# Four small changes at the start, middle and end of a fused attention and Fourier-mix kernel: row 0 loaded apart, batch 0 cast on two engines, batch 2 turned by DMA, the last tile stored 384 and 128 wide

## The chip, the cores and the metric

One core of one Trainium2 chip. The metric is the device time of one execution in microseconds (us). Before: 315.28 us median of 3 runs (315.26 to 315.30). The profile's span is about 1.8 us shorter than that time; times inside a profile count from the start of its span. All comparisons below use runs of the fast state (granted clock 0.99 to 1.00).

## The reference

```python
# x (8, 8, 512, 64) = batch, head, row, d; state (8, 8, 32, 64); w_ch1 (512, 2048); w_ch2 (2048, 512)
scores = x @ state^T / 8;  xread = softmax(scores) @ state        # 512 rows
scores2 = state @ x^T / 8; sread = softmax(scores2) @ x           # 32 rows
x = concat([xread, sread], rows) -> (8, 576, 512)                 # heads side by side
mixed = real(fft(fft(x, axis=1), axis=2))
u  = x + mixed
un = (u - mean(u)) / sqrt(var(u) + 1e-6)
out = u + relu(un @ w_ch1) @ w_ch2
# ... (cut: drawing of the inputs)
```

## The kernel before: what the change and the argument touch

The kernel writes one schedule for all engines by hand. A batch goes through these stages: load `x` and cast it to bfloat16 (`xin`), turn (transpose) it and the state (`xT`, `sT`), scores and exponentials, the reads (`XF`, `XR`, `XL`), the Fourier sums (`gp`, `yp`), `u` and its statistics, the turned `u` (`unT`), then the two matmul layers (`ph`, `po`), which are most of the time, and the store. Stages of the next batch are woven between the matmuls of the present one.

```python
    def load_x(b):                       # on SyncE's queue, two of batch 0's on ACT's
        ...
        for n, (ps, si, rows) in enumerate((
            (slice(0, 128), 2, xb[256:384]),
            (slice(0, 128), 0, xb[1:129]),
            (slice(0, 128), 1, xb[129:257]),
            (slice(0, 128), 3, xb[384:512]),
            (slice(0, 1), 2, xb[0:1]),           # overwrites partition 0 of the first load
        )): ...
    def cast_x(b):
        if b == 0:
            for si in (0, 1, 3, 2):
                nc.scalar.copy(t[:, si, 1:513], xs[:, si, :])
        else:
            nc.gpsimd.tensor_copy(t[:, :, 1:513], xs)
    # ... (cut)
    load_state(0, 1); load_x(0); load_state(1, 2); load_x(1)
    nc.sync.dma_start(out=s_dram[2:]..., in_=state[2:, :, ::-1, :]...)   # reversed state to HBM
    load_state(2, B, s_dram)                                            # SyncE waits for it here
    # ... (cut)
    x_by_dma, u_by_dma = 3, 2            # from which batch on x, and u, are turned by DMA
        def turn_x(g):
            if b >= x_by_dma:
                for si in ((0, 1), (3, 2))[g]:
                    nc.sync.dma_start_transpose(out=xT[:, :, 128 * si:128 * si + 128], in_=xin[:, si, 1:513])
                return
            ... # 8 transposes on TensorE, then
            (nc.vector.tensor_copy if b == 0 or g == 0 else nc.scalar.copy)(xT[:, 2 * g:2 * g + 2, :], ...)
        def turn_u(k, r):
            if b >= u_by_dma:
                nc.sync.dma_start_transpose(out=unT[:, :, col:col + 128], in_=ub[k, r])
                return
            ...
    # layer 2, the last tile of the last batch
                h = q // 2
                cols = slice(256 * h, 256 * h + 256)
                ... # 16 matmuls for each half, then DVE writes ot and SyncE stores it
    def warm(n):                         # idle matmuls: identity x identity into a tile nobody reads
        t = psF.tile([128, 512], F32, name="warm", tag="c")
        for i in range(n):
            nc.tensor.matmul(t[:, 0:128], lhsT=ident, rhs=ident, start=(i == 0), stop=(i == n - 1))
    # ... (cut) in the opening, while TensorE has nothing else to do:
    weave((warmed(s0[:1], 4) + warmed(s0[1:3], 2) + s0[3:], 0, 1), ...)
    weave((warmed(r0, 4), 0, 1), ..., ([lambda: warm(44)], 1, 1))
```

The softmax here doesn't subtract the row's maximum and nothing guards it: scores larger than these inputs give would overflow.

## Time and profile before

| | before |
|---|---|
| time | 315.28 us |
| span of the profile | 313.6 us |
| matmuls of TensorE, busy | 2320, 300.5 us (96%) |
| layer 1 of batch 0 starts | 28.65 us |
| first Fourier sum over d (yp) of batch 1 | 54.27 us |
| layer 1 of batch 2 starts | 91.85 us |
| start of the last 32 matmuls, end of the span | 306.51, 313.6 us |

Read it as a program that is bound by TensorE from about 42 us on, with a start of 42 us in which several engines hand work to each other, and an end of 3.5 us that no engine can overlap. The prediction shows the lines.

### The profile page before, as it was taken

What the parts mean: (1) busy time and instruction counts of PE and PEld (TensorE: products, weight loads), DVE (VectorE), ACT (ScalarE), POOL (GpSimd) and SP (SyncE); (2) the same over time, 40 slices, a digit from 0 to 9 for tenths busy, and PEclk for the clock granted to TensorE, in tenths of its full rate; (3) what the DMA queues carried; (4) which work ended last, traced back from release to release, by engine and by line L of the source; (5) the groups of instructions that cost most, each with busy time, mean ns of one, the idle gap of its engine ahead of it and who ended that gap; (6) DMA issues with size and microseconds to landing.
All of it is one profiled execution on the core that took longest, in us unless ns stands there. A gap on an engine that the chain in (4) does not pass through costs nothing.

```text
span 313.6 us, 5980 instructions
## 1 busy us (share of the span) xinstructions
PE 300.5 (96%) x2320; PEld 172.4 (55%) x2320; DVE 187.0 (60%) x445; ACT 138.5 (44%) x269; POOL 74.8 (24%) x170
## 2 busy tenths in 40 slices
PE   5878999999999999999999999999999999999995
PEld 5666997544544555456645554455445544555444
DVE  8796874968677593873817774686569563100012
ACT  6698765645543443243442444234533333333300
POOL 8658497320240040300600024002200131000000
PEclk9999999999999999999999999999999999999999
DMA  7997999466464925348434343631333034303155
GB/s 142 194 197 136 202 179 213 106 119 144 79 113 88 220 48 135 81 106 155 95 72 100 86 100 83 129 75 52 81 73 67 33 84 98 73 34 67 38 133 132
DMA packets 111532, 34.22 MB, mean 109 GB/s; under 512 B 102928, under 2 KB 107280, under 8 KB 111504
## 3 DMA queue, kind: packets, MB, share of 16 engines
q1 hardware_dynamic: 100784, 28.08, 43.1%
q0 software_dynamic: 4224, 4.19, 8.3%
q10 hardware_dynamic: 6496, 1.57, 2.4%
q8 instruction: 18, 0.29, 0.4%
q14 instruction: 10, 0.08, 0.1%
HBM read 22.43 MB, written 14.02 MB: 116 GB/s over the span
## 4 chain that ended last, share of the span: by engine, by line
PE 81%; DVE 12%; ACT 2%; DMA 2%; issue 1%; SPq 0%; DVEq 0%; ACTq 0%
PE po L762 32%; PE ph L696 29%; PE gp L576 3%; PE ph L706 3%; DMA xs<-in_x_dram 2%; DVE U L546 2%; DVE st L316 1%; PE yp L542 1%; PE po L754 1%; PE yp L541 1%; PE xfp L434 1%; PE xrp L434 1%; PE gp L580 1%; PE esp L409 1%; DVE XF L443 1%
## 5 line engine op out<-in xcount | busy, mean ns | idle before, releaser
L762 PE MATMUL po<-w,hT 128*128 128x512 bf16 x496 | 125.0, 379 | 0.0
L698 ACT ACTIVATE hT<-ph 128x512 bf16<-128x512 f32 x112 | 66.9, 597 | 123.7 <-PE ph L696 121.8
L696 PE MATMUL ph<-unT,w 128*128 128x512 bf16 x448 | 114.6, 379 | 0.4 <-DVE ot L727 0.3
L696 PEld LDWEIGHTS <-w 128*128 128x128 bf16 x576 | 51.1, 98 | 48.8 <-issue 1.3
L762 PEld LDWEIGHTS <-hT 128*128 128x128 bf16 x496 | 47.0, 98 | 44.3
L727 DVE SCALAR_TENSOR_TENSOR ot<-po,rstd,U 128x512 f32<-128x512 f32 (+1 forms) x33 | 24.2, 732 | 52.6 <-PE po L762 48.1
L586 POOL COPY GL<-G 128x128 bf16<-128x128 bf16 x8 | 2.4, 296 | 113.2 <-ACT G L584 113.2
L546 DVE TENSOR_TENSOR U<-yp,XR 128x512 f32<-128x512 f32 x16 | 10.9, 682 | 22.8 <-PE yp L542 22.8
L316 DVE BATCH_NORM_STATS2 st<-U 128x6 f32<-128x512 f32 x32 | 21.9, 683 | 0.1
L322 POOL TENSOR_TENSOR rstd<-mv,epst 128x1 f32<-128x1 f32 x34 | 7.1, 210 | 61.4 <-DVE mv L318 61.4
L323 POOL TENSOR_TENSOR rstd<-rstd,mhalf 128x1 f32<-128x1 f32 x34 | 20.9, 615 | 2.7
L584 ACT CAST G<-gp 128x288 bf16<-128x288 f32 x31 | 12.2, 397 | 12.0 <-PE gp L580 6.9
L706 PE MATMUL ph<-unT,w 128*128 128x128 bf16 x256 | 15.9, 219 | 0.7 <-ACT unT L620 0.7
L782 PE MATMUL warm<-ident 128*128 128x128 bf16 x152 | 12.8, 237 | 3.8 <-POOL ident masks.py:199 3.4
L706 PEld LDWEIGHTS <-w 128*128 128x128 bf16 x256 | 15.0, 98 | 0.9 <-issue 0.8
L782 PEld LDWEIGHTS <-ident 128*128 128x128 bf16 x152 | 11.1, 107 | 4.7 <-POOL ident masks.py:199 3.4
L576 PEld LDWEIGHTS <-XQ 128*128 128x128 bf16 x96 | 8.8, 98 | 8.8 <-DVE XQ L506 2.3
L136 POOL CAST xin<-xs 128x2048 bf16<-128x2048 f32 x7 | 13.2, 1891 | 0.3 <-issue 0.2
L610 DVE TENSOR_SCALAR ub<-U,mv 128x512 bf16<-128x512 f32 x24 | 12.3, 510 | 1.0 <-DVE mv L318 0.2
L434 PEld LDWEIGHTS <-ET 128*128 128x128 bf16 x80 | 7.0, 98 | 9.1 <-DVE XF L443 1.6
L443 DVE TENSOR_TENSOR XR<-xrp,rs 128x512 bf16<-128x512 f32 x16 | 11.1, 695 | 1.0 <-POOL XR L276 0.4
L708 ACT ACTIVATE hT<-ph 128x512 bf16<-128x512 f32 x16 | 9.3, 598 | 3.9 <-PE ph L706 3.9
(190 smaller groups left out, 356.5 us busy)
## 6 DMA issues: line engine op xcount, KB each, us to landing
xs<-in_x_dram SPq DMA_DIRECT2D x30, 256.0 KB, 5.3
w<-in_moe_w_ch_dram POOLq DMA_DIRECT2D x8, 512.0 KB, 11.6
out_dram<-ot SPq DMA_DIRECT2D x15, 256.0 KB, 3.6
r_dram<-ot SPq DMA_DIRECT2D x14, 256.0 KB, 2.2
out_dram<-r_dram SPq DMA_DIRECT2D x14, 256.0 KB, 3.7
xs<-in_x_dram ACTq DMA_DIRECT2D x2, 256.0 KB, 4.0
l_dram<-ot SPq DMA_DIRECT2D x2, 256.0 KB
r_dram<-ot ACTq DMA_DIRECT2D x2, 256.0 KB
```

The costliest lines, as they stand in the source:

```text
L316: nc.vector.bn_stats(st6, u)
L323: nc.gpsimd.tensor_tensor(rstd, rstd, mhalf, op=ALU.pow)
L434: nc.tensor.matmul(ph[:, 0:260], lhsT=ET[:, g, c0:c0 + 128], rhs=rhs, start=True, stop=True)
L443: nc.vector.tensor_tensor(ov, in0=p[ps, :, 0:256].rearrange("p g (h d) -> p g h d", d=D), in1=rs[ps].unsqueeze(3).to_broadcast([n, 2, 4, D ...
L546: nc.vector.tensor_add(u.rearrange("p (k r) -> p k r", r=2), p.rearrange("p (r k) -> p k r", r=2)[:, 0:u.shape[1] // 2, :], x.rearrange("p ...
L576: nc.tensor.matmul(p[:, 0:NM], lhsT=XQ[:, j, c, :], rhs=tab[c], start=(c == 0), stop=(c == 2 and j != 2))
L696: nc.tensor.matmul(ph[:, o:o + n], lhsT=w1[:, c, f * 128:(f + 1) * 128], rhs=un_of[key][:, c, :], start=(c == 0), stop=(c == DC - 1))
L698: nc.scalar.activation(hT[:, per * i:per * i + per, :].rearrange("p a b -> p (a b)"), ph, AF.Relu, scale=-1.0 if key in flipped else 1.0)
L706: nc.tensor.matmul(ph[:, o:o + 128], lhsT=w1[:, c, f * 128:(f + 1) * 128], rhs=un_of[key][:, c, 128 * r:128 * r + 128], start=(c == 0), st ...
L727: nc.vector.scalar_tensor_tensor(ot[:, cols], in0=po_of[i][:, 0:cols.stop - cols.start], scalar=rstd, in1=u[:, cols], op0=ALU.mult, op1=AL ...
L762: nc.tensor.matmul(po_of[i], lhsT=h_of[key][:, f, i * 128:(i + 1) * 128], rhs=w2[:, f, :], start=(f == 0), stop=(f == FC - 1))
L782: nc.tensor.matmul(t[:, 0:128], lhsT=ident, rhs=ident, start=(i == 0), stop=(i == n - 1))
```

## The change

Its intent: (1) row 0 of `x` need not wait for the landing of another load; (2) two engines cast batch 0; (3) TensorE, DVE and ACT are spared the turning of batch 2's `x` and state; (4) the last store, which nothing hides, is made smaller.

```diff
-            (slice(0, 128), 2, xb[256:384]),
+            (slice(32, 128), 2, xb[288:384]),
             ...
-            (slice(0, 1), 2, xb[0:1]),
+            (slice(2, 32), 2, xb[258:288]),
+            (slice(0, 2), 2, xb[0:258:257]),
@@
-            for si in (0, 1, 3, 2):
+            for si in (0, 1, 3):
                 nc.scalar.copy(t[:, si, 1:513], xs[:, si, :])
+            nc.gpsimd.tensor_copy(t[:, 2, 1:513], xs[:, 2, :])
@@
-    x_by_dma, u_by_dma = 3, 2
+    x_by_dma, u_by_dma = 2, 2
@@
-            (nc.vector.tensor_copy if b == 0 or g == 0 else nc.scalar.copy)(
+            (nc.vector.tensor_copy if g == (b == 0) else nc.scalar.copy)(
@@
-                h = q // 2
-                cols = slice(256 * h, 256 * h + 256)
+                cols = slice(0, 384) if q < 2 else slice(384, 512)
@@  (the width of the matmuls follows cols)
-    ... [last_sines, exp_again, last_loads, load_x3,
+    ... [last_sines, exp_again, last_loads, turned[2], load_x3,
-    ... (scores_next, 0.26, 0.9) ...
+    ... (scores_next, 0.4, 1) ...
```

More of the change, by code (lines that the diff above doesn't have):

```diff
@@ L753, in step @@
                 for f in range(8 * (q % 2), 8 * (q % 2) + 8):
-                    nc.tensor.matmul(po_of[i][:, 0:256], lhsT=h_of[key][:, f, i * 128:(i + 1) * 128], rhs=w2[:, f, cols],
+                    nc.tensor.matmul(po_of[i][:, 0:cols.stop - cols.start], lhsT=h_of[key][:, f, i * 128:(i + 1) * 128], rhs=w2[:, f, cols],
                                      start=(f == 0), stop=(f == FC - 1))
@@ L797 @@
     turns1, copies1, s1 = s1[0], s1[1:4], s1[4:]
-    for step in (warmed(t0[:2], 2) + [alternate, more_loads] + warmed(t0[2:4], 2) + [last_sines, exp_again, last_loads, load_x3,
+    for step in (warmed(t0[:2], 2) + [alternate, more_loads] + warmed(t0[2:4], 2) + [last_sines, exp_again, last_loads, turned[2], load_x3,
             t0[4], t0[8], W(6), turns1, t0[5], W(10), t0[7], copies1[0], copies1[1], t0[6], copies1[2],
@@ L804 @@
     weave((L[11:], 0, 0.25), (t1, 0.2, 1), ([M[i] for i in (0, 4, 1, 5, 2, 6, 3, 7, 8, 9)], 0.33, 0.99),
-          ([lambda: state_blocks(3, B, nc.gpsimd.tensor_copy)], 0.35, 0.35), (scores_next, 0.26, 0.9), ([lambda: load_x(4)], 0.6, 0.6))
+          ([lambda: state_blocks(3, B, nc.gpsimd.tensor_copy)], 0.35, 0.35), (scores_next, 0.4, 1), ([lambda: load_x(4)], 0.6, 0.6))
     l2 = M
```

## The prediction

> **What bounds the kernel now.** I read the page first (busy shares, slices), then the chain that ended last in order of time, then the timeline of the opening, of 42 to 85 us and of the end, then the SyncE queue's waits. From the page:
>
> ```profile
> PE 300.5 (96%) x2320; PEld 172.4 (55%) x2320; DVE 187.0 (60%) x445; ACT 138.5 (44%) x269; POOL 74.8 (24%) x170
> ...
> PE   5878999999999999999999999999999999999995
> ```
>
> TensorE is the bound from about 42 us to the end, at a clock of 1.000. Only the first 42 us (5, 8, 7, 8 tenths), a DVE stretch at 54 to 62 us and the last slice have slack. All four parts of the change sit there, so each is judged by the chain of its own stretch. Opening, from the timeline:
>
> ```profile
> 8.22 1.66 ACT L134 CAST xin<-xs 128x512 bf16<-128x512 f32 x3 [0.62 <-DMA xs<-in_x_dram]
> ...
> 8.64 0.56 DVE L228 TENSOR_TENSOR gen<-gen 128x384 f32<-128x384 f32 x1
> ...
> 9.23 0.56 DVE L201 SCALAR_TENSOR_TENSOR gen<-gen 128x384 f32<-128x384 f32 x1
> ...
> 9.85 0.19 POOL L272 COPY gate<-gen 128x4 f32<-128x4 f32 x1 [1.18 <-DVE gen L201]
> ...
> 10.48 3.26 POOL L288 DMA_DIRECT2D w<-in_moe_w_ch_dram  x4 [0.19 <-issue]
> ...
> 13.93 0.70 DVE L443 TENSOR_TENSOR XR<-xrp,rs 128x512 bf16<-128x512 f32 x1 [0.41 <-POOL XR L276]
> ...
> 14.73 1.28 ACT L464 ACTIVATE XR<-srp,rcs 32x64 bf16<-32x64 f32 x4 [0.93 <-DVE rcs L455]
> ```
>
> There are two chains here, not one. One is x: load, four casts on ACT to 9.88, turn, copy, scores, exponentials to 13.81. The other is DVE's tables to 9.79, then GpSimd's gate, four w1 issues, its clear of XR (ends 13.90), DVE's XR, the reciprocal at 14.54, ACT from 14.73. From 14.73 ACT works without a gap through its sines, which end at 23.06; GpSimd then clears a row of TO and casts batch 1 (23.82 to 25.72), and TensorE waits for that cast (0.15 us, at 25.77). So the second chain, not x, sets 25.77 us. The middle, from the chain that ended last:
>
> ```profile
> 42.47 6.25 PE ph L706 x112
> 48.72 0.37 PE gp L576 x3
> 49.09 0.22 PE sTp L361 x4
> ...
> 51.28 0.45 PE xTp L373 x8
> 51.73 0.86 PE po L762 x4
> 52.59 0.37 PE gp L576 x3
> 52.96 0.45 PE xTp L373 x8
> 53.40 0.86 PE po L762 x4
> 54.27 0.11 PE yp L541
> ```
>
> TensorE is gapless up to yp at 54.27, and DVE's adds and statistics of batch 1 wait for yp. Turning batch 2 stands on this path. DMA and the end:
>
> ```profile
> SPq L108 <- DMA s_dram<-in_state_dram: 15.9, 1, 15.9
> ...
> 306.51 3.51 PE po L754 x32
> 310.01 0.02 issue
> 310.04 0.48 DVE ot L727
> ```
>
> SyncE stands still 15.9 us until the reversed state is in HBM (28.31), and only then issues the load of batch 2. The end is matmul, 0.48 us of DVE, then a store, the program's close at 313.6.
>
> **What the Trainium skill says.** "SBUF — State Buffer", section "Who interferes with whom": DVE and GpSimd share a port pair as an exclusive lock; a DVE instruction with two SBUF inputs and a GpSimd instruction that reads SBUF block each other whole. The trace agrees: DVE's L496, 0.43 us at 19.85, took 1.27 us at 43.94 beside GpSimd's L495 (43.53 to 44.93). "DMA: Bandwidth & Descriptors", section "Queues, rings and completion order": each engine goes round its queues packet by packet. The trace agrees: from 43 to 51 us about 150 packets of 256 bytes (x of batch 3) and 150 of 1024 bytes (w2) went per us, so a loading transfer of small packets crawls beside w2. The same page, "DMA Transpose (X-bar)": TensorE's way goes through PSUM, the DMA's from SBUF to SBUF by SyncE or ACT. The trace's batches 3 to 7 do it so: 1.27 us of issue and 2.5 us to landing each when nothing else runs.
>
> **Part 1, row 0 without overwriting.** It removes the wait of row 0's load for the whole third block (issued at 6.19, after the block's landing at 6.17). But ACT waits only for the second block, which lands at 8.20; row 0 landed at 8.27 and the cast that needs it began at about 9.3. Bytes are the same, so the last byte of x lands at about 8.1 either way. Gain on the path: 0. Off the path SyncE runs ahead: the DMA engines, at a share of 0.08 from 7 to 8 us, stay fed, batch 1 is down by about 12 us and not 14.4, before w1 begins to compete; the state copy then starts about 2.4 us earlier, ends near 26, and batch 2 is loaded, gated and cast some 2.5 us earlier (cast end 41.94 becomes about 39.3).
>
> **Part 2, the cast on two engines.** ACT's last cast ends at about 9.0 in place of 9.88. GpSimd's cast of 512 columns: 1.89 us for 2048 and 0.34 us for 128 (L155) give 0.34 + 384 x 0.81 ns = 0.65 us. GpSimd is free at 8.67, but DVE then holds L228 (two SBUF inputs) to 9.20. GpSimd slips in there, casts to about 9.85, and L201 runs to about 10.4 in place of 9.79. The copy of xT's first half moves to ACT (1.0 us and not 0.7) and the other stays on DVE: score exponentials end at 13.5 to 14.0, against 13.81. That is not the bound. But the gate, w1's issue and the clear of XR hang on L201: the second chain is 0 to 0.6 us later, and so is 25.77. I take +0.3.
>
> **Part 3, batch 2 turned by DMA.** TensorE loses 20 transposes: 0.22 + 0.45 + 0.45 = 1.12 us before yp. DVE loses 0.42 (sT) and 0.69, ACT 1.01. The order of the steps is respread: the first scores (0.23 us) now stand ahead of yp. So yp comes 1.12 - 0.23 = 0.89 us earlier, and DVE's chain behind it, which leads to layer 1 of batch 1 at 65.3, comes along. The last score turns move behind one more turn of u; this may free part of the 0.63 us that TensorE waits at 61.6; I take 0.2. New cost: the first scores need all six transposes. TensorE reaches them at 48.72 + 0.37 + 0.37 + 0.86 + 0.74 + 0.86 + 0.37 = 52.3 us. Transposes can start at about 39.3; w2 is then running (an estimate from its 12.4 us at 97 ns a packet). Four xT of 512 packets and two sT of 256 are 160 a DMA engine. If each waits for one w2 packet (105 ns a round), 80 are done when w2 ends at 48.5, the rest take 3 us more, and the landing 1: 52.5 to 53. If they are not interleaved so, 48 to 49. Expected stall: 0.2 us. Loads of batches 3 and 4 now stand behind them in the queue, and land near 58 and 62; batch 3's cast at 62.57 has room.
>
> **Part 4, the last tile.** Matmul columns stay (16 x 512), 3.51 us. The last store shrinks from 256 to 128 columns: DVE, 0.75 us for 512 and 0.48 for 256, gives about 0.34 for 128; half the bytes save about 0.15 in transfer. The 384 columns are ready at 309.1, added by 309.8, and drain before. Gain 0.3.
>
> **Sum.** +0.3 - 0.9 - 0.2 + 0.2 - 0.3 = -0.9 us. 315.28 - 0.9 = 314.4.
>
> **Rivals.** (a) The transposes come late: should the state copy not end earlier (its last landings straggle from 26.1 to 28.3), they begin at 42, end near 55, and TensorE stands 2.5 us at the first scores: 316.5. The packets' fair share speaks for it, SyncE's freed queue against. (b) The port lock is the larger thing: GpSimd and DVE lose 0.6 us, the transposes are in time: 314.7. For it: GpSimd's L94 to L97, one column wide, took up to 1.05 us beside DVE's table steps. (c) x was the bound after all and the opening gets 0.6 to 1 us shorter, as one reads from the chain, which runs through the casts: then 313.2. Against it: ACT's 0.93 us wait at 14.73, for DVE and not for x. (d) Batch 1's stretch gains more, as DVE and ACT lose 2.1 us of copies near it: 313.5; against it DVE sat idle 1.94 and 2.35 us just there.
>
> **Range and chances.** Rivals (c) and (d) together give about 312.8, (a) in half its size 315.8. Range 312.9 to 315.7. A change of 2% is 6.3 us; all gains together are 3, the worst wait that I see is 3. So within 2% is nearly sure: 0.97, faster 0.02, slower 0.01.
>
> **What would show it.** Right: TensorE's wait for the cast of batch 1 stays at 25.8 to 26.4; DVE's L201 ends after 10.2; batch 2's load is issued before 27; no wait of TensorE on xT or sT over 0.6 us; yp of batch 1 about 0.6 us earlier; the last DVE piece 0.34. Wrong: layer 1 of batch 0 starting over 0.5 us earlier than 28.65, or a wait of over 1 us at the first scores of batch 2.

## The result

| | before | after |
|---|---|---|
| time, median of 4 runs each on one chip | 315.29 us (315.26 to 315.33) | 315.31 us (314.99 to 315.69) |
| ratio | | 1.0001, 95% interval 0.9984 to 1.0018 |
| span of the profile | 313.6 us | 313.9 us |

A ratio here is the mean time of one kernel's fast runs over that of the other's of the same rounds, so it is not quite the ratio of the medians. The time did not move. The profiled execution of the kernel after is its slowest of four, so its trace ends 0.3 us later than before, and the four runs spread ten times as wide as before's.

The kernel after has the same TensorE bound (page of the profile, busy shares and slices):

```profile
PE 299.2 (95%) x2300; PEld 170.2 (54%) x2300; DVE 185.0 (59%) x442; ACT 137.6 (44%) x268; POOL 75.0 (24%) x171
...
PE   5778999999989999999999999999999999999995
```

There are 20 matmuls fewer, as intended, and the twelfth slice (86 to 94 us) is no longer full. To see where the time goes, I set the starts of the same steps side by side and follow the offset, after minus before: +0.21 us at layer 1 of batch 0, -0.78 at layer 1 of batch 1, +0.29 at layer 1 of batch 2, +0.27 at the start of the last matmuls, +0.30 at the end. So the middle did gain 0.99 us, and 1.07 us were lost in one place, at layer 1 of batch 2.

**Opening** (timeline of the kernel after: start, length, what, idle before and what ended it):

```profile
8.60 1.14 ACT L135 CAST xin<-xs 128x512 bf16<-128x512 f32 x2 [1.08 <-DMA xs<-in_x_dram]
...
8.99 0.68 POOL L136 CAST xin<-xs 128x512 bf16<-128x512 f32 x1 [0.32 <-DMA xs<-in_x_dram]
9.23 0.85 DVE L203 SCALAR_TENSOR_TENSOR gen<-gen 128x384 f32<-128x384 f32 x1
...
10.14 0.19 POOL L274 COPY gate<-gen 128x4 f32<-128x4 f32 x1 [0.47 <-DVE gen L203]
...
15.02 2.56 ACT L466 ACTIVATE XR<-srp,rcs 32x64 bf16<-32x64 f32 x8 [1.02 <-DVE rcs L457]
```

DVE's step took 0.85 us beside GpSimd's cast, and 0.56 before; the gate, 9.85 before, is at 10.14, and ACT's step, 14.73 before, at 15.02. **SyncE** waits less for the reversed state (waits of SyncE's queue):

```profile
SPq L108 <- DMA s_dram<-in_state_dram: 12.9, 1, 12.9
```

That wait ended at 24.73 us and not 28.31; batch 2's load was issued at 25.74 and not 28.94, its cast ended at 39.19 and not 41.94. **Middle** (the chain that ended last, kernel after):

```profile
48.93 0.73 PE gp L578 x6
49.67 0.86 PE po L763 x4
...
52.50 0.23 PE esp L411 x8
52.73 0.86 PE po L763 x4
53.59 0.11 PE yp L543
```

The turns of state and `x` (sTp, xTp) are gone from the chain, the first scores (esp) stand in it without a wait, and yp comes at 53.59 in place of 54.27. **Layer 1 of batch 2**: among the waits of TensorE stands one that before has not,

```profile
PE ph L698 <- DMA unT<-ub: 1.1, 1, 1.1
```

and the timeline of TensorE shows it, first before, then after:

```profile
91.85 1.02 PE L696 MATMUL ph<-unT,w 128*128 128x512 bf16 x4
```

```profile
92.14 1.02 PE L698 MATMUL ph<-unT,w 128*128 128x512 bf16 x4 [1.06 <-DMA unT<-ub]
```

It waits for a DMA that the change does not touch: the turning of batch 2's `u`. Four such transposes go through SyncE's queue. The timeline of SyncE has the third of them so, before and after:

```profile
87.85 1.19 SPq L615 DMA_TRANSPOSE unT<-ub  x1
```

```profile
86.92 2.48 SPq L617 DMA_TRANSPOSE unT<-ub  x1
```

The third was issued 0.93 us earlier, held SyncE 1.29 us longer, and so the fourth, whose input had been ready at 88.69 us, was issued at 89.52 and landed at 92.00, 0.28 us later than before (91.72). Before, the landing was 0.13 us ahead of its use. In all twelve fast traces (before, after and ten of the runs below) layer 1 of batch 2 starts 0.13 or 0.14 us after the fourth landing, whether a wait is listed or not, so that landing sets the start in every kernel and the stage had no slack at all; what TensorE gained in the middle it stood here. What held the third up? The DMA queues in two stretches, 85 to 87 us before and 87 to 89 us after (queue, packets, MB, share of 16 engines' time):

```profile
q8 instruction: 1, 0.02, 3.0%
```

```profile
q8 instruction: 1, 0.02, 4.2%
```

Queue q8 carries instructions, in 18 packets of 16384 bytes over the program, each 0.9 to 1.8 us on one of the 16 DMA engines. The trace's records place this packet at 85.60 us before, where it held up the second transpose (2.12 us on SyncE; there was time to spare), and at 87.63 after, 0.71 us behind the issue of the third. (A second instruction queue, q14, with packets of 8192 bytes, is not the cause: before had one at 88.01 us, 0.16 us behind the issue of the third, which took its usual 1.19.)

**End.** The last step of DVE is shorter as planned (0.35 and 0.48 us), yet nothing was gained. The chain that ended last, kernel after:

```profile
306.78 3.51 PE po L755 x32
310.29 0.03 issue
310.31 0.35 DVE ot L729
```

From the end of DVE to the landing of the last store it took 1.73 us before and 2.26 after. The timeline shows another write, issued on ACT's queue just ahead of it, before and after:

```profile
307.22 0.56 ACTq L743 DMA_DIRECT2D out_dram<-r_dram  x1
```

```profile
308.73 0.56 ACTq L745 DMA_DIRECT2D out_dram<-r_dram  x1
```

It came 1.51 us later, since it stands behind another such write, which waited for its source; 15 of that source's 16 landings were there by 303.21, and one at 304.47; the source had been issued at 300.70, and an instruction packet began at 300.88 (before: 296.87, well ahead of the issue at 300.42).

### The profile page after: what moved, and what is told of

Its sections match the earlier page's. It is cut to its first block, busy times and chain, and to the rows that moved or that the text cites. A ratio compares the mean times of both kernels' runs of the same rounds, so it can differ in the third digit from the quotient of the medians.

```text
span 313.9 us, 5948 instructions
## 1 busy us (share of the span) xinstructions
PE 299.2 (95%) x2300; PEld 170.2 (54%) x2300; DVE 185.0 (59%) x442; ACT 137.6 (44%) x268; POOL 75.0 (24%) x171
## 4 chain that ended last, share of the span: by engine, by line
PE 76%; DVE 15%; DMA 3%; ACT 3%; issue 1%; SPq 0%; DVEq 0%; ACTq 0%
PE po L763 31%; PE ph L698 27%; PE gp L578 3%; PE ph L708 3%; DVE U L548 3%; DVE st L318 2%; DMA xs<-in_x_dram 2%; DVE ub L612 1%; PE po L755 1%; PE xfp L436 1%; PE yp L544 1%; DVE ot L729 1%; PE xrp L436 1%; PE gp L582 1%; PE yp L543 1%
## 5 line engine op out<-in xcount | busy, mean ns | idle before, releaser
L729 DVE SCALAR_TENSOR_TENSOR ot<-po,rstd,U 128x512 f32<-128x512 f32 (+2 forms) x33 | 24.1, 732 | 52.2 <-PE po L763 47.9
```

The lines of the kernel that those rows point to most:

```text
L729: nc.vector.scalar_tensor_tensor(ot[:, cols], in0=po_of[i][:, 0:cols.stop - cols.start], scalar=rstd, in1=u[:, cols], op0=ALU.mult, op1=AL ...
```

## The experiments

Two theories for the loss at layer 1 of batch 2. **A**: the instruction packet feeds TensorE, and the number of instructions ahead of a point decides when it comes; 20 matmuls fewer in the middle moved it by 2 us from a harmless transpose onto the one without slack. **B**: the change's own traffic, batch 2's transposes and the loads behind them, delays `u`. A later rival, **C**: idle matmuls in the opening are worth time by themselves. Twelve kernels ran, all correct. "Before" in those runs had 315.35 us median.

**e1_fetch_back**: the kernel after, with 20 idle matmuls more in the opening, so that the count is before's.

```diff
-    weave((warmed(s0[:1], 4) + ...
+    weave((warmed(s0[:1], 20) + ...
-    ... ([lambda: warm(44)], 1, 1))
+    ... ([lambda: warm(48)], 1, 1))
```

> The changed kernel with 20 more matmuls of the idle kind (16 behind the first turning of the state, 4 behind the 44), all where TensorE waits in the opening, so that its instruction stream is as long ahead of 50 us as in the kernel before. Theory A (TensorE's instruction packets of 16384 bytes, one in about 128 matmuls, were moved by the 20 matmuls fewer onto the third DMA transpose of batch 2's u, whose issue then took 2.48 us and not 1.19): the packet near 87.6 us leaves that place, the wait of 1.06 us at layer 1 of batch 2 goes, time 315.3 - 1.0 = 314.3, or 314.0 if the end recovers its 0.3 too. Rival B (SyncE's queue is later for other reasons: six loads a batch and not five, or loads of batches 3 and 4 behind the transposes): the wait stays, 315.3, or later by up to 0.3 for the added matmuls.

Measured: fast runs 314.25, 314.27, 314.40 and 315.10 us, ratio 0.9973 (0.9960 to 0.9986). Matmuls that compute nothing gave back about 1 us; A stands so far, B alone cannot explain it. But e5 and e6 below, with the same 20 matmuls, did not show this gain, so e1 proves little by itself.

**e2_before_less20**: the kernel before, with 20 idle matmuls fewer, nothing else.

```diff
-    ... ([lambda: warm(44)], 1, 1))
+    ... ([lambda: warm(24)], 1, 1))
```

> The kernel before with 24 idle matmuls in place of 44 at 17.7 us: less work, nothing else changed. Theory A: the instruction packet near 85.6 us comes some 16 to 20 matmuls later in the work, near 88.4 us, onto the third or fourth transpose of batch 2's u: layer 1 of batch 2 waits 0.5 to 1.1 us and the time rises to 315.8 to 316.4. Rival B: 315.3 or a little below.

Measured: 316.52 us (316.11 to 318.10), ratio 1.0049 (1.0031 to 1.0067). Among TensorE's waits:

```profile
PE ph L696 <- DMA unT<-ub: 0.6, 1, 0.6
```

The packet came at 88.23 us, the third transpose took 1.96 us. Doing less work made the kernel before slower, at the place that A names, with none of the change in it. That is the strongest run for A. The profiled execution is 0.88 us longer than before: 0.62 at this place, and 0.25 at the end, where another packet met a store (below).

**e3_no_dma_turn**: the kernel after without part 3, 2320 matmuls.

```diff
-    x_by_dma, u_by_dma = 2, 2
+    x_by_dma, u_by_dma = 3, 2
-    ... last_loads, turned[2], load_x3, ... (scores_next, 0.4, 1)
+    ... last_loads, load_x3, ... (scores_next, 0.26, 0.9)
```

> The changed kernel with batch 2 turned by TensorE again, at the old places of its score steps: parts 1, 2 and 4 alone. Theory A: opening 0.21 later as measured, instruction packets as in the kernel before, end 0.0 to 0.3 earlier: 315.2 to 315.5. Rival B with six loads a batch as the cause: the wait at layer 1 of batch 2 appears here too, about 316.4.

Measured: 315.22 us, ratio 0.9999 (0.9986 to 1.0012). Opening +0.23, packet at 85.83 and no wait for `unT`, +0.09 behind batch 2, and the end 0.17 earlier than before: parts 1, 2 and 4 together give nothing, the loss in the opening cancelling the gain at the end (0.26).

**e4_dma_turn_only**: the kernel before with part 3 alone (the same three places the other way), 2300 matmuls.

> The kernel before with batch 2 turned by DMA and its score steps at their new places: part 3 alone. If loading row 0 without a wait is what brings batch 2 down early enough, then here the transposes begin only near 42 us beside w2, land at 53 to 55, and TensorE stands 1 to 3 us at the first scores of batch 2: 316 to 317.5. If part 3 needs no help: yp of batch 1 0.9 us earlier than before, then the wait at layer 1 of batch 2 as in the changed kernel: 315.1 to 315.3.

Measured: 315.12 us (314.76 to 315.85), ratio 0.9995 (0.9983 to 1.0007). Middle gain 0.88, no stall at the first scores (this was expected at 1 to 3 us, and missed: the first sT landed at 51.81, the scores began at 52.09), and a wait of 0.73 us for `unT`, with the packet at 87.37. So part 3 alone brings both the gain and the loss.

**e5_fetch_back_casts_act** (e1 with part 2 undone) and **e6_fetch_back_halves** (e1 with part 4 undone):

```diff
@@ e5, against e1
-            for si in (0, 1, 3):
+            for si in (0, 1, 3, 2):
-            nc.gpsimd.tensor_copy(t[:, 2, 1:513], xs[:, 2, :])
-            (nc.vector.tensor_copy if g == (b == 0) else nc.scalar.copy)(
+            (nc.vector.tensor_copy if b == 0 or g == 0 else nc.scalar.copy)(
@@ e6, against e1
-                cols = slice(0, 384) if q < 2 else slice(384, 512)
+                cols = slice(0, 256) if q < 2 else slice(256, 512)
```

> The changed kernel with the 20 idle matmuls of the run before, and the cast of batch 0 and the copies of its turned x as they were (part 2 undone). If GpSimd's cast beside DVE's L203 (port pair held in turn) makes the opening 0.2 us later: first matmul of layer 1 back at 28.65 in place of 28.86, time 0.2 below that of the first run, 314.2; instruction packet near 85.5 us, no wait at layer 1 of batch 2. If part 1 (six loads, earlier state copy) is the cause of the 0.2: 28.86 and 314.4.

> The changed kernel with the 20 idle matmuls, and the last tile stored in two halves of 256 (part 4 undone): 0.2 to 0.3 more than the first run, 314.6, if the narrower last store is worth what the run without DMA turning showed at its end (0.26); the same as the first, 314.4, if it is worth nothing.

Measured: e5 314.94, 314.97, 315.00 and 315.79 us in its fast runs, ratio 0.9994 (0.9981 to 1.0007): a miss, and its profiled run was slow, so I can only argue why. e6 315.31 us (314.95 to 315.35), ratio 0.9996 (0.9983 to 1.0009): a miss of both outcomes. Its trace shows that 20 idle matmuls were not free: layer 1 of batch 0 began 0.72 us later than before, since the turns of `x` waited behind them. Twenty was too many. But e1 has the same 20 and ran in 314.3 us; part 4 (0.3 us, e10) cannot make up the 1.0 us between e1 and e6, so the gap stays unexplained.

**e7_ten_more**: the kernel after with ten idle matmuls more, 2310 in all.

```diff
-    weave((warmed(s0[:1], 4) + ...
+    weave((warmed(s0[:1], 14) + ...
```

> The changed kernel with 10 idle matmuls more in place of 20. Theory A (instruction packets): the packet comes to lie between its places in the changed kernel (87.6) and with 20 (about 85), near 86 to 87; a wait at layer 1 of batch 2 of 0 to 0.7 us, time 314.3 to 315.1, with more spread between runs than with 20. If the 20 matmuls help by something else that grows with their number (a warmer TensorE): half of it, 314.85, with no relation to the packet's place.

Measured: 314.34 us (314.26 to 314.58), ratio 0.9969 (0.9957 to 0.9981). In the timeline of TensorE:

```profile
91.37 1.02 PE L698 MATMUL ph<-unT,w 128*128 128x512 bf16 x4 [0.25 <-DMA unT<-ub]
```

The packet came at 86.45 us, 0.51 us ahead of the third transpose, which then took 1.19 us. The offset behind batch 2 is -0.48, the end -1.12. The ten were free here: opening +0.23, as without them. The wider spread that was expected did not come.

**e8_parts_3_4_fetch_back**: the kernel before with parts 3 and 4 and the 20 idle matmuls of e1, so without parts 1 and 2 (the edits are those of e1, e4 and the change's own for part 4).

> The kernel before with part 3 and part 4 and the 20 idle matmuls, without parts 1 and 2: opening as before, layer 1 of batch 1 0.9 us earlier, no wait at layer 1 of batch 2, end 0.2 to 0.3 earlier: 315.35 - 1.15 = 314.2. If the gain needs part 1 or 2: 314.6 or more.

Measured: 315.38 us (314.49 to 316.11), ratio 1.0000. TensorE's waits hold a new one:

```profile
PE esp L409 <- DMA sT<-stb: 1.6, 1, 1.6
```

The transposes began at 41.91 us (kernel after: 39.21), the first of the two sT landed at 54.31, the scores began at 54.44. The state copy varies: SyncE's wait for it ended at 28.51 here and at 27.08 in e4, where there was no stall. But the DMA queues from 51 to 53 us hold another cause:

```profile
q8 instruction: 1, 0.02, 3.4%
```

An instruction packet began at 51.76 us. The landings of the fourth xT straggle from 52.55 to 53.82 there, while in the seven other traces with part 3 they took 0.1 us or less. In e12 (below), whose transposes began at 41.59, nearly as late, no packet fell there and the wait was 0.37 us. So most of the 1.6 us is very likely the packet's; no run moves only it. Nor is the rest of e8 clean: the 20 idle matmuls made its opening 0.59 us late, and the profiled run is its slowest of six.

Does part 1 give part 3 its room? With parts 1 and 2 SyncE's wait ended at 24.5 to 25.5 us (after, e3, e6, e7, e10), with part 1 and not part 2 at 26.88 (e11), without either at 27.1 to 28.5 (six traces). No run has part 1 alone; that it helps is likely, its size is not shown.

**e9_before_less10**: the kernel before with ten idle matmuls fewer.

```diff
-    ... ([lambda: warm(44)], 1, 1))
+    ... ([lambda: warm(34)], 1, 1))
```

> The kernel before with 10 idle matmuls of the opening fewer (2310 in all). Theory A (the place of the instruction packet decides): with 2320 matmuls the packet came at 85.60 us, with 2300 at 88.23; so with 2310 at about 86.9, between the second and the third of the four turns of batch 2's u, which then take 1.2 us each as far as they are issued alone; TensorE waits under 0.3 us for the last of them and the time is 315.3 to 315.5. Theory C (fewer idle matmuls cost by themselves, say through the start of the opening): the loss is about half of the 1.2 us that 20 fewer cost, 315.9 to 316.0.

Measured: 315.39 and 315.41 us. The packet came at 87.28, 0.59 us ahead of the third transpose, which took 1.19 us; every offset to before is 0.01 us or less. So ten fewer cost nothing, and 20 fewer cost 1.2: C, which wanted half, falls.

**e10_ten_more_halves**: e7 with part 4 undone (the edit of e6).

> The kernel after with ten idle matmuls more (the best so far, 314.34 us) and part 4 undone: halves of 256 for the last tile. If part 4 is worth its 0.3 us once the packet of the end is out of the way: 314.6 to 314.7, with the last step of DVE at 0.48 us and the end 0.3 us later against the start of the last matmuls. If part 4 is worth nothing in this kernel (the last store ends at the same time, since it starts later in one case and is larger in the other, or the other stores set the end): 314.3.

Measured: 314.65 us (314.54 to 314.70), ratio 0.9977 (0.9962 to 0.9991); against e7's 314.34 part 4 is worth 0.31 us of the medians (the intervals of the two ratios overlap). In the profiles the end differs by 0.27 us, as planned; another 0.15 comes from the opening (+0.38, against +0.23), whose code is the same in both.

**e12_turn_and_ten**: the kernel before with part 3 alone (the edit of e4) and ten idle matmuls more (the edit of e7).

> The kernel before with part 3 alone (batch 2 turned by DMA) and ten idle matmuls more, so 2310 in all. Part 3 alone had 315.12 us with a wait of 0.7 us for the turned u of batch 2. If that wait is the packet's, it goes and the time is 314.3 to 314.6, with yp of batch 1 about 0.9 us earlier than before and no wait of TensorE for unT over 0.3 us. If part 3 alone has too little time for its transposes (part 1 being what gives it room), a wait of 0.5 us or more for sT stands at the first scores of batch 2 and the time is 315 or more.

Measured: 313.80, 313.89, 314.76 and 315.63 us, median 314.33, ratio 0.9974 (0.9956 to 0.9991). No wait for `unT`; a wait for sT of 0.37 us in the profiled run (314.76), with transposes from 41.59 us. There yp of batch 1 came no earlier than before, where 0.9 us was expected. One part of the four gives as much as all with ten idle matmuls (e7), in the median, but with a spread of 1.8 us, which I put down to the transposes' missing room (inferred; only one of the four was profiled).

**e11_ten_more_casts_act**: e7 with part 2 undone (the edit of e5).

> The kernel after with ten idle matmuls more (314.34 us) and part 2 undone: all four casts of batch 0 on ACT, the copies of xT on DVE. If part 2 is what makes the opening 0.2 us later (DVE's step on the gate's path takes 0.85 us beside GpSimd's cast, and 0.56 us without it): layer 1 of batch 0 starts at 28.6 to 28.7 in place of 28.9, and the time is 314.1. If another thing sets the opening (the first loads, the idle matmuls): layer 1 of batch 0 stays at 28.85 or later and the time is 314.3 or more.

Measured: 314.03 us (313.98 to 314.49), ratio 0.9961 (0.9949 to 0.9974): the best median of all. But the start of layer 1 of batch 0, expected at 28.6 to 28.7, was 28.81. The timeline of its opening:

```profile
9.23 0.56 DVE L202 SCALAR_TENSOR_TENSOR gen<-gen 128x384 f32<-128x384 f32 x1
...
11.80 1.20 ACT L401 ACTIVATE ET<-eTp 128x512 bf16<-128x512 f32 x2 [1.28 <-PE eTp L399]
```

DVE's step is back at 0.56 us and the gate at 9.86, as before; the exponentials of the scores, 11.64 before, now come 0.16 later, and so does everything behind them. Two chains of the opening stand within a few hundredths: in e4 the exponentials came 0.26 us earlier than before, and layer 1 of batch 0 only 0.04. Part 2 lengthens one chain, ten idle matmuls the other. With 0.15 us between two traces of one opening (e7 and e10), the 0.07 us of e11 against e7 says little by itself, and the intervals of their ratios overlap. The rest of e11's gain over e7 is at layer 1 of batch 2, which waited for nothing.

Eight of the traces at that place, in the order of the packet relative to the third transpose (transpose: issue, time on SyncE):

| kernel | matmuls | packet at | transpose that it met | fourth landed | TensorE waited |
|---|---|---|---|---|---|
| before | 2320 | 85.60 | 2nd: 84.88, 2.12 us | 91.72 | 0 |
| e3 | 2320 | 85.83 | 2nd: 85.12, 2.08 us | 91.80 | 0 |
| e9 | 2310 | 87.28 | none (3rd: 87.87, 1.19 us) | 91.73 | 0 |
| e7 | 2310 | 86.45 | none (3rd: 86.96, 1.19 us) | 91.23 | 0.25 |
| e11 | 2310 | 86.55 | 3rd, a little: 86.88, 1.45 us | 90.91 | 0 |
| e2 | 2300 | 88.23 | 3rd: 87.83, 1.96 us | 92.33 | 0.65 |
| e4 | 2300 | 87.37 | 3rd: 86.79, 2.19 us | 91.54 | 0.73 |
| after | 2300 | 87.63 | 3rd: 86.92, 2.48 us | 92.00 | 1.06 |

The other four agree: in e6 and e8 the packet met the second transpose (0.47 us behind its issue and 0.09 ahead of it: 1.82 and 1.90 us), in e12 and e10 it began 0.52 and 0.34 us ahead of the third (1.19 and 1.22 us). So a packet that began between 0.1 us ahead of a transpose's issue and 0.7 us behind it held it up by 0.6 to 1.3 us; one that began half a microsecond ahead did not. Waits of 0.22 to 0.25 us in e6, e7 and e10, where the third was hardly held up, say that the stage is at its edge anyhow.

The same holds over the whole program. The twelve fast traces (all runs but e1 and e5, before and after included) have 288 transposes of `u`. A packet of q8 began between 0.1 us ahead of the issue and 0.8 us behind it in 19 of them, and 18 of these took 1.61 to 2.95 us (the exception, in e3 at 155.23 us, took 1.19). The other 269 took at most 1.45.

**The end, settled from these traces.** Before, the last store landed at 312.25 us on the first of the eight DMA semaphores that SyncE waits for at the close, and the eight waits then followed one another every 0.06 us; from landing to the end of the span 1.35 us. In all eight traces with part 3 the last store sits on the last but one, and it took 0.97 or 0.98; in all four without (before, e2, e3, e9), 1.34 or 1.35. Six more DMA issues on SyncE have turned the rotation of the eight semaphores; part 1's eight more alone (e3) left the last store on the first. So part 3 gave 0.37 us there that nobody had planned. Part 4 gave 0.13 us of DVE and 0.13 of transfer (from DVE's end to landing 1.60 us in e3 and e7, 1.73 or 1.74 in before, e10 and e12). The late write has a packet behind it in each trace that shows it: in after, e2 and e4, all with 2300 matmuls, a q8 packet began 0.18 to 0.47 us behind the issue of its source, whose last landing then came 1.0 to 1.3 us behind the fifteenth, and the last store took 2.26, 1.98 and 2.01 us. In the nine others the packet had ended before that issue and the last landing was at most 0.16 us behind. In the kernel after the sum is +0.27 (start of the last matmuls) - 0.13 + 0.53 (the store beside the late write) - 0.37 = +0.30.

## Why the prediction was right, and where it was not

The time, 315.31, lies in the range and within 2%. The middle of the range, 0.9 us of gain, did not come. That the range held is partly luck: no rival in it names what happened, a gain of 0.99 us taken back at a place that the prediction did not look at. Two of its sums do not come out: rivals (c) and (d), 1.2 and 0.9 us below 314.4, make 312.3 and not 312.8, and half of (a), 1.05 above, makes 315.45 and not 315.8.

1. **Part 1** (gain 0 by itself, SyncE ahead): right as far as it goes. Issue of batch 2's load before 27 us, cast end 39.19 (said 39.3); but in e11, without part 2, these were 27.55 and 39.88, so part of it was not part 1's. One thing the other way: in this trace `x`'s second block landed later, at about 8.6 us and not at 8.2; in the others with part 1 it was 8.1 to 8.4.
2. **Part 2** (+0.3 in the opening, through DVE's step and the gate): right in mechanism, +0.21. GpSimd's cast took 0.68 (said 0.65); DVE's step ended at 10.08, so the sign "after 10.2" was missed: the prediction let the whole 0.56 us follow the cast, 9.67 + 0.56 = 10.23; it lost 0.29 us and not 0.6. In the five traces where the two meet (after, e3, e6, e7, e10) the step ended 0.41 or 0.42 us after the cast, whether it took 0.85 or 1.01: it waited for the end of the cast, and 0.15 of its 0.56 us lay outside the wait. That the second chain "and not x" sets the start was too sharp: e4 and e11 show both within 0.05 us.
3. **Part 3** (-0.9, -0.2, +0.2): right in sum, -0.99. yp came 0.68 us earlier (sign given: about 0.6), and no stall at the first scores. Rival (a)'s stall came in runs without part 1: 0.37 us in e12; the 1.6 us of e8, and 0.17 us in e6, which has part 1, came with an instruction packet (51.76 and 50.78 us).
4. **Part 4** (-0.3): the worth was right, 0.26 to 0.31 in e3 and in e10 against e7, but the kernel after did not get it: the store took 0.53 us longer beside a write that came 1.51 us late.
5. **The sum**: this is the step that failed. It ended with the opening, the middle and the tail, on the ground that TensorE "is the bound from about 42 us to the end", so that what is gained carries through. But layer 1 of batch 2 starts when the DMA-turned `u` has landed, and before, that was 0.13 us ahead of its use: no slack, which no list of waits shows. Taking 20 matmuls out moved an instruction packet onto that transpose, and 1.07 us, all that the middle had gained, came back as a wait (0.8 of it goes with the packet; 0.25 stays in e7). With the packet elsewhere (e7) the gain is 1.12 us in the profile and 1.0 in the time, close to the predicted 0.9, though that sum has 0.37 us of the close in it which I had not foreseen, and 0.26 of loss at batch 2.

What the Trainium skill says on such packets: "Runtime: NRT & Kernel Launch", section "Instruction fetch mechanics": an engine's instructions are refilled in blocks of 16 KiB, 256 instructions, over the sequencer's own DMA queue, at a cost that is "mostly hidden". The trace agrees on the block (18 packets of 16384 bytes) and the lists of TensorE's waits name no packet; but on a DMA engine that also serves a transpose it went with a wait of TensorE of up to 1.06 us. That the packets are TensorE's is inferred from the count (2320 matmuls with as many weight loads fill 18 blocks of 256) and from their moving with it; the trace does not name the engine. The count holds in all twelve fast traces: on average one packet in 248 to 254 matmuls and weight loads of TensorE, and the packet near 87 us came when 1696 to 1716 of them had started.

**Open.** e1 and e5 have no fast trace. e5's 0.8 us miss could come from the 20 idle matmuls, which delay the score chain in e6; but e1 has them too and is 0.7 to 1.0 us faster than e5 and e6, so that this is not explained. A rests on e2, e7, e9 and the traces, not on e1. The spread of the kernel after (0.7 us against 0.07) fits packets that fall now on one moment, now on another, but only one run of each kernel is profiled. That the packet at 300.88 us caused the late landing at 304.47 fits all twelve fast traces; of these e9 and e2, which differ by ten idle matmuls alone, lie on either side.

## What to carry to other kernels

Before you credit a gain on the bound engine to the end, look for the next place where that engine meets a transfer, and measure the slack there (landing to use), not only the waits: zero slack looks like no wait. When a small edit moves the time in a place that it does not touch, compare the instruction packets of the DMA queues in both traces; ten matmuls that compute nothing, where TensorE is idle anyhow, tell you whether their place is the cause. And undo the parts of a bundle one at a time under the mended condition: here one part of four carried the gain (part 3), one perhaps gave it room (part 1), one was worth 0.3 us at the end (part 4), and without part 2 the median was 0.3 us lower still.

## What the Trainium skill lacked or had wrong

- "Runtime: NRT & Kernel Launch", section "Instruction fetch mechanics": it calls the cost of a block "mostly hidden" and looks only at the engine that is fed. Here one packet took 0.9 to 1.8 us on its DMA engine and held a DMA transpose's 1.2 us on SyncE for 1.96 to 2.48 us; TensorE waited 0.65 to 1.06 us, and 20 matmuls fewer made the kernel before 1.2 us slower. Over the twelve traces 18 of 19 such meetings lengthened a transpose of `u` to 1.61 us or more.
- "DMA: Bandwidth & Descriptors", section "DMA Transpose (X-bar)": it gives no time for transposes beside other traffic. Six of batch 2 took from 39.21 to 52.22 us to land beside w2's load, where one of batch 2's `u` lands 2.4 us after its issue.
- "SBUF — State Buffer", section "Who interferes with whom": it does not say how much of an instruction lies outside the wait. Here DVE's step of 0.56 us ended 0.41 or 0.42 us after GpSimd's cast in five traces, so 0.15 us of it did.
- In none of the pages that I read: the order of the closing waits. The last store on the first semaphore waited for, in place of the last but one, cost 0.37 us (1.35 and 0.98 us from landing to end).
